# Second MLP layer of an FNet block as seven products, with the MLP in two passes and its activations in DRAM

## The chip, the cores and the metric

The kernel runs on one core of a Trainium2 chip. The core has TensorE (PE in the profile; PEld is its loading of weights), VectorE (DVE), ScalarE (ACT), GpSimd (POOL, which this kernel does not use for computing) and SyncE (SP, which here only issues DMAs). SBUF is the on-chip memory of 128 partitions; PSUM has eight banks, each of 512 float32 per partition, into which PE accumulates. The metric is the time of one execution in microseconds (us) on the device; lower is better.

## The reference

S = 2048 rows, D = 512, F = 1792, all float32.

```python
xn = layernorm(x)                       # over D
a = xn @ dft_hid_re.T;  b = xn @ dft_hid_im.T
s = dft_seq_re @ a - dft_seq_im @ b     # the FNet mixing
h = relu(xn @ w1 + b1) ** 2             # (2048, 1792)
out = x + s * silu(h @ w2 + b2)
```

## The kernel before

**Precision.** Every matmul operand is cut into a high part, rounded to PE's fast float32 type (`split`, L51: ACT copies, DVE subtracts the copy from the source), and a low part. A product is three passes, high x high, high x low, low x high (`PASSES`).

**Seven products.** A product of two operands, each cut 2 x 2 into blocks, takes seven block products in place of eight, if sums of blocks are formed first and the seven results are combined afterwards (`PRODUCTS`, `ORDER`). The kernel uses this for the sequence DFT of c = 2 to 7 (L476 to L516) and for the first MLP layer (`hidden`, L404), not for the second (`outer`, L439).

**Order of the work.** First layernorm, beside the plain sequence DFT of c = 0 and 1 (L286). Then six steps of c, each of eight j-steps: seven products of six matmuls of 256 columns (`mm`, L219), the moving operand being made two j-steps ahead (`prep`, `moving`); in j = 2, 3 the hidden DFT of the c before (`stage2`, L206), whose result y goes to DRAM. At j = 7 the seven PSUM banks are recombined by DVE into four blocks, cut into the buffers pq00 to pq11, from which `stage2` reads. Between, jobs prepare the weights (`make_w1`, `make_w2`): load, sums, cuts into the pq buffers, and DMA to DRAM.

Then the MLP in one pass over 28 units (c, p): four quarters c of 512 rows and seven pairs p of feature blocks. A unit is `hidden` (42 matmuls of 256 columns into four banks; recombination, Relu and square on DVE; cut on ACT and DVE) and, one unit behind, `outer`: 2 feature blocks x 4 row tiles x 3 passes = 24 matmuls of 512 columns, accumulated over all p in four PSUM banks. After the last p, `finish` adds b2, applies Silu, multiplies with y, adds x and writes the rows out. In the last quarter the end of the accumulation runs row tile by row tile (`REST`), the last row tile in two halves.

**What sets the order.** The code is traced in program order; a scheduler of the framework then puts each engine's instructions in an order of its own by their readiness, an instruction with earlier place first. Engines run their queues in order and wait on semaphores. A buffer is named by its tag: `buf("g1", ..., bufs=2)` is a tile in one of two buffers of tag g1, and a tile can be written when all readers of the tile that held the buffer are done, DMAs out of it included.

## Time and profile before

| | |
|---|---|
| median of three runs | 732.88 us (732.64 to 734.16) |
| the profiled execution | 733.41 us, span 731.5 us |
| PE busy | 721.0 us, 99% of the span |
| DVE busy | 547.6 us, 75% |
| ACT busy | 255.2 us, 35% |
| DMA | 133.70 MB, mean 183 GB/s |
| mean granted TensorE clock | 0.996 |

The span is the time from the first to the last instruction of the profiled execution, whose own time is 1.9 us longer. The DFT steps of c = 2 to 7 lie between 112.6 and 418.8 us and take 51 us each; the MLP runs from 418.8 us to the end. In rows of the profile, `out<-in` are tiles by their names with numbers left out, so `m<-g,xc` are the seven products of the DFT, `hps` those of the first MLP layer, `ops` the accumulators of the second; `128x512` is partitions by elements, x28 a count, then come the busy time in us, the mean of one in ns, and the idle time of the engine before them with what ended it.

### The profile page before, as it was taken

How to read it: one execution, taken by the hardware profiler on the slowest of the kernel's cores; microseconds unless marked ns; L12 is line 12 of the kernel's file. 1: busy time of each engine (PE TensorE's matmuls, PEld its weight loads, DVE VectorE, ACT ScalarE, POOL GpSimd, SP SyncE). 2: the span in 40 equal slices, each digit the busy share in tenths (PEclk: the TensorE clock that was granted, in tenths of full speed). 3: DMA queues.
4: the chain of work that ended last, by engine and by line, in shares of the span. 5: the costliest groups of instructions: out<-in, count | busy, mean ns of one | idle time of the engine just before them, and what ended most of it. 6: DMA issues, size and time to landing. Idle time of an engine off the chain costs nothing.

```text
span 731.5 us, 11771 instructions
## 1 busy us (share of the span) xinstructions
PE 721.0 (99%) x4687; PEld 654.1 (89%) x4687; DVE 547.6 (75%) x976; ACT 255.2 (35%) x386; POOL 0.2 (0%) x4
## 2 busy tenths in 40 slices
...
GB/s 301 231 88 86 211 77 87 148 298 117 234 255 91 288 188 111 307 137 127 289 135 149 360 425 288 151 167 86 231 207 139 95 226 184 143 73 288 116 116 59
DMA packets 43335, 133.70 MB, mean 183 GB/s; under 512 B 5008, under 2 KB 7312, under 8 KB 40592
## 3 DMA queue, kind: packets, MB, share of 16 engines
...
## 4 chain that ended last, share of the span: by engine, by line
PE 94%; DMA 2%; DVE 2%; ACT 1%; issue 1%; SPq 0%; DVEq 0%; ACTq 0%
PE m L219 33%; PE ops L441 19%; PE hps L414 17%; PE pq L309 13%; PE yps L206 12%; DMA w<-w2d 1%; DMA out<-fin 1%; DMA r<-in_ct 1%; DVE fin L457 0%; DVE fin L456 0%; ACT hh L52 0%; ACT g L52 0%; ACT z L455 0%; DVE z L454 0%; ACT xc L52 0%
## 5 line engine op out<-in xcount | busy, mean ns | idle before, releaser
L219 PEld LDWEIGHTS m<-g,xc 128*128 128x128 f32 x2016 | 242.6, 189 | 2.1
L219 PE MATMUL m<-g,xc 128*128 128x256 f32 x2016 | 243.2, 281 | 0.0
L441 PE MATMUL ops<-w,hh 128*128 128x512 f32 (+1 forms) x714 | 161.7, 381 | 0.4 <-ACT hh L52 0.3
L441 PEld LDWEIGHTS ops<-w,hh 128*128 128x128 f32 x714 | 126.5, 188 | 26.3 <-ACT hh L52 0.8
L414 PEld LDWEIGHTS hps<-xT,w 128*128 128x128 f32 x1008 | 123.3, 190 | 2.3
L414 PE MATMUL hps<-xT,w 128*128 128x256 f32 x1008 | 124.3, 281 | 0.0
L52 ACT ACTIVATE g<-r 128x768 fp32r<-128x768 f32 (+2 forms) x65 | 57.2, 888 | 128.9 <-PE m L219 99.3
L53 DVE TENSOR_TENSOR g<-r,g 128x768 fp32r<-128x768 f32 (+2 forms) x65 | 65.1, 1008 | 44.4 <-ACT g L52 44.2
L309 PE MATMUL pq<-g,xc 128*128 128x512 f32 x384 | 92.2, 400 | 3.7 <-ACT xc L52 3.7
L206 PE MATMUL yps<-wd,pq 128*128 128x512 f32 x384 | 94.1, 395 | 0.0
L309 PEld LDWEIGHTS pq<-g,xc 128*128 128x128 f32 x384 | 72.9, 190 | 22.4 <-ACT xc L52 4.5
L206 PEld LDWEIGHTS yps<-wd,pq 128*128 128x128 f32 x384 | 70.3, 188 | 15.1
L52 ACT ACTIVATE hh<-h 128x512 fp32r<-128x512 f32 x56 | 34.1, 630 | 116.4 <-DVE h L431 116.4
L53 DVE TENSOR_TENSOR g<-t,g 128x1024 fp32r<-128x1024 f32 x48 | 58.2, 1222 | 3.5 <-ACT g L52 3.3
L422 DVE SCALAR_TENSOR_TENSOR h<-hps,b1s,ht 128x256 f32<-128x256 f32 x28 | 13.5, 481 | 57.1 <-ACT ht L419 57.1
L52 ACT ACTIVATE g<-t 128x1024 fp32r<-128x1024 f32 x48 | 50.0, 1051 | 2.6 <-PE pq L309 2.6
L53 DVE TENSOR_TENSOR hh<-h,hh 128x512 fp32r<-128x512 f32 x56 | 36.8, 688 | 4.5 <-ACT hh L52 2.8
L431 DVE SCALAR_TENSOR_TENSOR h<-h 128x512 f32<-128x512 f32 x56 | 36.6, 685 | 0.3
L419 ACT ACTIVATE ht<-hps 128x256 f32<-128x256 f32 x28 | 10.7, 382 | 68.0 <-PE hps L414 68.0
L162 DVE TENSOR_TENSOR t<-r 128x512 f32<-128x512 f32 x48 | 32.5, 686 | 1.1 <-DMA r<-in_ct 0.8
L52 ACT ACTIVATE xT<-stage 128x768 fp32r<-128x768 f32 (+1 forms) x16 | 15.3, 955 | 45.8 <-DVE stage L248 28.2
L164 DVE TENSOR_TENSOR t<-r,t 128x256 f32<-128x256 f32 x48 | 19.8, 420 | 0.6
...
## 6 DMA issues: line engine op xcount, KB each, us to landing
r<-in_ct SPq DMA_DIRECT2D x63, 512.0 KB, 3.4
w<-w2d SPq DMA_DIRECT2D x28, 512.0 KB, 4.0
w<-w2d SPq DMA_DIRECT2D x14, 1024.0 KB, 4.8
w1d<-w1g SPq DMA_DIRECT2D x21, 512.0 KB, 4.2
...
w2d<-w2g SPq DMA_DIRECT2D x14, 512.0 KB, 5.2
...
stage<-in_xt SPq DMA_DIRECT2D x8, 512.0 KB, 5.2
```

The source lines that it names most:

```text
L52: cut[0] = nc.scalar.activation(hi, src, AF.Copy)
L53: return nc.vector.tensor_tensor(lo, src, hi.bitcast(F32), op=ALU.subtract)
L162: nc.vector.tensor_tensor(t[:, 0:2], r[:, I12:I12 + 1].to_broadcast([P, 2, CW]), r[:, I11:I22 + 1], op=ALU.subtract)
L164: nc.vector.tensor_tensor(t[:, 2], r[:, I22], t[:, 0], op=ALU.subtract)
L206: nc.tensor.matmul(ps, PQ[c, m, k // 2][:, a_, w:w + P], WD[m, k][:, b_, :], start=n == 0, stop=n == 2 * ND * 3 - 1)
L219: nc.tensor.matmul(ps[:, d * CW:(d + 1) * CW], w[:, a_, d * P:(d + 1) * P], mv(b_), start=first and d == 0 and (a_, b_) == (HI, HI), stop= ...
L309: nc.tensor.matmul(accs[k], w, g[:, b_, 2 * h:2 * h + 2], start=j == 0 and h == 0 and (a_, b_) == (HI, HI), stop=j == NJ - 1 and h == 1 an ...
L414: nc.tensor.matmul(M[n], W1[p][a][:, a_, q * P:(q + 1) * P], xT[c, q][:, b, b_], start=i == q == 0 and (a_, b_) == (HI, HI), stop=q == 1 a ...
L419: nc.scalar.activation(u, M[1], AF.Copy)
L422: nc.vector.scalar_tensor_tensor(h0[:, 0:256], M[2], c0, u, op0=ALU.add, op1=ALU.add)
L431: nc.vector.scalar_tensor_tensor(r, r, 0.0, r, op0=ALU.max, op1=ALU.mult)
L441: ins = nc.tensor.matmul(ps, H[c, f][:, a_, t * P:(t + 1) * P], W2[c, f][:, b_, cols], start=f == 0 and (a_, b_) == (HI, HI), stop=f == NF ...
```

## The change

- The second layer uses seven products too. Row halves and feature pairs of h, and feature pairs and column halves of w2, are the 2 x 2 blocks. Per unit: 7 products x 2 row tiles x 3 passes, 42 matmuls of 256 columns, into seven PSUM banks that accumulate over p; b2 is written by ACT into three of the banks before the accumulation (`bias`).
- The MLP runs in two passes. Pass one computes `hidden` for all 28 units, with Relu (with b1) and Square on ACT, and writes h to DRAM (HD), 512 KB a unit. For p = 6 (`EARLY`) the sums and cuts are made at once, and the cut operand is written from buffers g0a and g1a. Pass two loads each unit's h two units ahead (`outer_operand`), into g1a or g1b in turn, forms the sums, cuts all seven blocks into xc3, wd0 or wd1 in turn, and runs `outer`. A unit of p = 6 is loaded ready cut. W2 is read once, in the last quarter of pass one, into the xc buffers.
- Recombination (`combine`) works on pairs of products at once, so PSUM is split by tags: b3 (three banks), b2 (two), ba, bb and bc (one each), each a single buffer. DFT steps use b2, b3, ba, bb; `stage2` uses bc and comes in j = 1, 2.
- Weight jobs (`make_w`) are now 14 alike, at j = 2, 4, 6 (`JOBS`). They use a buffer e, which the recombination uses too.
- The halves of the next quarter's MLP input (`xt_half`) are made in three parts spread over units of pass one. At the end, the last quarter runs its last three p product by product.

```diff
-REST = NF - 3
+REST = NP - 3
+EARLY = (6,)
+JOBS = {2: (2, 4, 6), 3: (2, 4, 6), 4: (2, 4, 6), 5: (2, 4, 6), 6: (2, 4)}
...
-    acc = ctx.enter_context(tc.tile_pool(name="acc", bufs=8, space=bass.MemoryType.PSUM))
+    acc = ctx.enter_context(tc.tile_pool(name="acc", bufs=1, space=bass.MemoryType.PSUM))
...
-    def bank(name):
-        return acc.tile([P, 512], F32, tag="bank", name=name)
-    def t2k(name):
-        return pool.tile([P, 512], F32, tag="t2k", bufs=4, name=name)
+    def bank(tag, name):
+        n = {"b3": 3, "b2": 2}.get(tag, 1)
+        return acc.tile([P, n, 512], F32, tag=tag, name=name)
...
+    def sums_b(t, r):
+        nc.vector.tensor_tensor(t[:, 0:2], r[:, 0:1].to_broadcast([P, 2, 256]), r[:, 1:3], op=ALU.add)
+        nc.vector.tensor_tensor(t[:, 2], t[:, 1], r[:, 1], op=ALU.add)
+        nc.vector.tensor_tensor(t[:, 3], t[:, 2], r[:, 3], op=ALU.add)
+    def sums_a(t, a21, a11_a22, a11, a12):
+        nc.vector.tensor_tensor(t[:, 0:2], a21.to_broadcast([P, 2, 256]), a11_a22, op=ALU.subtract)
+        nc.vector.tensor_tensor(t[:, 2], t[:, 1], a11, op=ALU.subtract)
+        nc.vector.tensor_tensor(t[:, 3], t[:, 2], a12, op=ALU.add)
...
-        g0 = buf("g0", [P, 2, 3, CW], f"g0_{key}", F32R, bufs=2)
-        g1 = buf("g1", [P, 2, 4, CW], f"g1_{key}", F32R, bufs=2)
+        k = "ab"[turn[0] % 2]
+        turn[0] += 1
+        g0 = buf(f"g0{k}", [P, 2, 3, CW], f"g0_{key}", F32R)
+        g1 = buf(f"g1{k}", [P, 2, 4, CW], f"g1_{key}", F32R)
...
+    def banks(key):
+        m26, m753, m4, m1 = (bank(tag, f"m_{tag}_{key}") for tag in ("b2", "b3", "ba", "bb"))
+        return m26, m753, m4[:, 0], m1[:, 0]
+    def product(ms, n):
+        m26, m753, m4, m1 = ms
+        return {1: m1, 4: m4, 2: m26[:, 0], 6: m26[:, 1], 7: m753[:, 0], 5: m753[:, 1], 3: m753[:, 2]}[n]
+    def combine(e, ms):
+        m26, m753, m4, m1 = ms
+        pair = [P, 2, m1.shape[-1]]
+        nc.scalar.activation(e[:, 0], m1, AF.Copy)
+        nc.vector.tensor_tensor(e[:, 1:3], m26, e[:, 0:1].to_broadcast(pair), op=ALU.add)
+        nc.vector.tensor_tensor(e[:, 0:4:3], m753[:, 0:2], e[:, 2:3].to_broadcast(pair), op=ALU.subtract)
+        nc.vector.tensor_tensor(e[:, 2:4], m753[:, 1:3], e[:, 0:4:3], op=ALU.add)
+        if m4 is not None:
+            nc.vector.tensor_tensor(e[:, 0], m4, e[:, 0], op=ALU.subtract)
...
+        both = r.rearrange("p (k h) n -> p k (h n)", k=2)
+        for m, op in ((0, ALU.subtract), (2, ALU.mult)):
+            mr = xT["rows"][:, m:m + 2].rearrange("p h n -> p (h n)")[:, None, :]
+            nc.vector.tensor_tensor(both, both, mr.to_broadcast([P, 2, 512]), op=op)
+        yield
+        sums_b(t, r)
+        yield
+        g = xT[c, q] = buf(f"xc{q}" if c % 2 == 0 else f"wd{q}", [P, 2, 7, 256], f"xT{c}_{q}", F32R)
+        split(g[:, HI, 0:3], g[:, LO, 0:3], r[:, I11:I21 + 1])
+        split(g[:, HI, 3:7], g[:, LO, 3:7], t)
+        yield
...
+    def make_w(n, p):
+        e = buf("e", [P, 8, 256], f"w{n}raw{p}")
+        r, t = e[:, 0:4], e[:, 4:8]
+        nc.sync.dma_start(r, (w1, w2)[n][p])
+        if n == 0:
+            sums_a(t, r[:, 0:1], r[:, 1:4:2], r[:, 1], r[:, 2])
+        else:
+            sums_b(t, r)
+        for k, (first, count) in enumerate(((0, 2), (2, 1), (3, 2), (5, 2))):
+            g = buf(f"pq{k // 2}{k % 2}", [P, 2, count, 256], f"w{n}g{p}_{k}", F32R)
+            split(g[:, HI], g[:, LO], e[:, 1 + first:1 + first + count])
+            nc.sync.dma_start((W1D, W2D)[n][p][:, :, first:first + count], g.bitcast(F32))
+    work = [(0, p) for p in range(NP)] + [(1, p) for p in range(NP)]
+    jobs = {(c, j): work.pop(0) for c, js in JOBS.items() for j in js}
...
+    def load_w2(p):
+        t = W2[p] = buf(f"xc{(0, 1, 4, 5, 6, 7, 2)[p]}", [P, 2, 7, 256], f"w2_{p}", F32R)
+        nc.sync.dma_start(t.bitcast(F32), W2D[p])
...
+    def room(n, name):
+        return buf("r" if n % 4 < 3 else "sx", [P, 4, 256], name, bufs=3 if n % 4 < 3 else 1)
+    def hidden_sums(x_):
+        h = x_[:, 4:8]
+        sums_a(x_[:, 0:4], h[:, C12:C12 + 1], h[:, C11:C22 + 1], h[:, C11], h[:, C21])
+    def hidden(n, c, p):
+        if n % 2:
+            t, o = bank("b3", f"hps{n}_3"), bank("bc", f"hps{n}_1")
+            t = t.rearrange("p a (b n) -> p (a b) n", n=256)
+            ms = t[:, 0:2], t[:, 2:5], t[:, 5], o[:, 0, 0:256]
...
+            t, u, o = (bank(tag, f"hps{n}_{tag}") for tag in ("b2", "ba", "bb"))
+            t, u = (v.rearrange("p a (b n) -> p (a b) n", n=256) for v in (t, u))
+            ms = u, t[:, 0:3], t[:, 3], o[:, 0, 0:256]
+            order = ORDER if n else (1, 7, 5, 3, 4, 2, 6)
+        first = set()
+        for k in order:
+            a, b = W1_SLOT[PRODUCTS[k][0]], B_SLOT[PRODUCTS[k][1]]
+            share = next((pair for pair in ((2, 6), (7, 5), (3, 4)) if k in pair), k)
+            for q in range(2):
+                for a_, b_ in PASSES:
+                    nc.tensor.matmul(product(ms, k), W1[p][a][:, a_, q * P:(q + 1) * P], xT[c, q][:, b_, b],
+                                     start=share not in first, stop=q == 1 and (a_, b_) == (LO, HI),
+                                     skip_group_check=True)
+                    first.add(share)
+        early = buf("e", [P, 8, 256], f"h{c}_{p}") if p in EARLY else None
+        x_ = room(n, f"h{c}_{p}") if early is None else early[:, 4:8]
+        combine(x_, ms)
+        for f, s in ((2 * p, slice(C11, 4, 2)), (2 * p + 1, slice(C21, 4, 2))):
+            nc.scalar.activation(x_[:, s], x_[:, s], AF.Relu, bias=b1s[:, f:f + 1])
+        nc.scalar.activation(x_, x_, AF.Square)
+        if early is None:
+            nc.sync.dma_start(HD[c, p], x_)
+            return
+        hidden_sums(early)
+        for s, tag in ((slice(4, 7), "g0a"), (slice(0, 4), "g1a")):
+            g = buf(tag, [P, 2, s.stop - s.start, 256], f"h{tag}{c}_{p}", F32R)
+            split(g[:, HI], g[:, LO], early[:, s])
+            nc.sync.dma_start(HD[c, p][:, :, s], g.bitcast(F32))
+    def outer_operand(n, c, p):
+        g = buf(("xc3", "wd0", "wd1")[n % 3], [P, 2, 7, 256], f"g{c}_{p}", F32R)
+        if p in EARLY:
+            nc.sync.dma_start(g.bitcast(F32), HD[c, p])
+        else:
+            x_ = buf("g1" + "ab"[n % 2], [P, 8, 256], f"hr{c}_{p}")
+            nc.sync.dma_start(x_[:, 4:8], HD[c, p])
+            hidden_sums(x_)
+            split(g[:, HI], g[:, LO], x_[:, 0:7])
+        return g
+    BIASED = {2: 0, 5: 1, 4: 0}
...
+    def outer(m, n, g, p, cols=(0, 1)):
+        a, b = H_SLOT[PRODUCTS[n][0]], B_SLOT[PRODUCTS[n][1]]
+        for k in cols:
+            for a_, b_ in PASSES:
+                nc.tensor.matmul(m[:, k * 256:(k + 1) * 256], g[:, a_, a, k * P:(k + 1) * P], W2[p][:, b_, b],
+                                 start=p == 0 and k == 0 and (a_, b_) == (HI, HI) and n not in BIASED,
+                                 stop=p == NP - 1 and (a_, b_) == (LO, HI), skip_group_check=True)
...
+    def finish(c, e, first, count, cols=slice(0, 2)):
+        m, i = first // 2, first % 2
+        w = slice(cols.start * 256, cols.stop * 256)
+        z = e[:, first:first + count, w]
+        y, xr = (fin[c][2 * n + m][:, i:i + count, w] for n in range(2))
         nc.scalar.activation(z, z, AF.Silu)
-        nc.vector.tensor_tensor(y, z, y, op=ALU.mult)
-        nc.vector.tensor_tensor(y, y, xr, op=ALU.add)
-        nc.sync.dma_start(out[n * P:(n + 1) * P, cols], y)
+        nc.vector.tensor_tensor(z, z, y, op=ALU.mult)
...
+        if j in (1, 2):
+            stage2(c - 1, j - 1)
         if (c, j) in jobs:
-            make, arg = jobs[c, j]
-            make(arg)
+            make_w(*jobs[c, j])
         if j == NJ - 1:
-            u = t2k(f"m1_{c}")
-            nc.scalar.activation(u, M[1], AF.Copy)
-            c11 = t2k(f"c11_{c}")
-            nc.vector.tensor_tensor(c11, M[2], u, op=ALU.add)
-            nc.vector.tensor_tensor(u, M[6], u, op=ALU.add)
-            u3 = t2k(f"u3_{c}")
-            nc.vector.tensor_tensor(u3, M[7], u, op=ALU.add)
-            nc.vector.tensor_tensor(u, M[5], u, op=ALU.add)
-            c22 = t2k(f"c22_{c}")
-            nc.vector.tensor_tensor(c22, M[5], u3, op=ALU.add)
-            nc.vector.tensor_tensor(u, M[3], u, op=ALU.add)
-            nc.vector.scalar_tensor_tensor(u3, M[4], -1.0, u3, op0=ALU.mult, op1=ALU.add)
-            pq(c, 0, 0, c11)
-            pq(c, 1, 1, c22)
-            pq(c, 1, 0, u)
-            pq(c, 0, 1, u3)
+            e = buf("e", [P, 4, 512], f"c{c}")
+            combine(e, ms)
+            for m, dh, k in ((0, 0, C11), (1, 1, C22), (1, 0, C12), (0, 1, C21)):
+                pq(c, m, dh, e[:, k])
...
+    for n, (c, p) in enumerate(units):
+        hidden(n, c, p)
+        if n == 0:
+            stage2(NC - 1, 0)
+            stage2(NC - 1, 1, "ba")
+        if c == 0 and p + 4 < NP:
+            load_w1(p + 4)
+        if c + 1 < NTC and p < 6:
+            if p % 3 == 0:
+                making = xt_half(c + 1, p // 3)
+            next(making)
+        if c == NTC - 1:
+            if p == 0:
+                load_w2(0)
+                load_w2(1)
+            if p < 5:
+                load_w2(p + 2)
+    ready = {}
+    for n, (c, p) in enumerate(units[:2]):
+        ready[c, p] = outer_operand(n, c, p)
     for n, (c, p) in enumerate(units):
         last = c == NTC - 1
         if p == 0:
-            po = [(t, cols, bank(f"ops{c}_{t}_{cols.start}")[:, 0:cols.stop - cols.start])
-                  for t in range(TPC)
-                  for cols in ([slice(0, 256), slice(256, D)] if last and t == TPC - 1 else [slice(0, D)])]
-        if c == 0 and p + 4 < NP:
-            load_w1(p + 4)
-        if n + 1 < len(units):
-            load_w2(*units[n + 1])
-        if not last and p in (3, 4):
-            xt_half(c + 1, p - 3)
-        if p == 5:
-            for t in range(TPC):
-                load_fin(c * TPC + t)
-        if n + 1 < len(units):
-            if last and p + 1 >= NP - 2:
-                places = buf(f"xc{p + 3 - NP}", [P, 2, 2, TC], f"hh{p + 1}", F32R)
-                hidden(*units[n + 1], [places[:, i] for i in range(2)])
+            ms = banks(f"o{c}")
+            for k in BIASED:
+                if last and k == 4:
+                    m4 = bank("bc", "m4_last")[:, 0], ms[2]
+                    for i in range(2):
+                        bias(m4[i], k, slice(i, i + 1))
+                else:
+                    bias(product(ms, k), k)
+        if p == 2:
+            load_fin(c)
+        if n + 2 < len(units):
+            ready[units[n + 2]] = outer_operand(n + 2, *units[n + 2])
+        def add(k, p):
+            if last and k == 4:
+                for i in range(2):
+                    outer(m4[i], k, ready[c, p], p, (i,))
             else:
-                hidden(*units[n + 1])
-        for f in (2 * p, 2 * p + 1):
-            if not last or f < REST:
-                for t, cols, ps in po:
-                    tail = outer(ps, c, f, t, cols)
+                outer(product(ms, k), k, ready[c, p], p)
+        if not last or p < REST:
+            for k in ORDER:
+                add(k, p)
         if p == NP - 1:
-            z = buf("g0", [P, 3, 512], f"z{c}", bufs=2)
-            for t, cols, ps in po:
-                if last:
-                    for i in range(REST, NF):
-                        with tc.issue_after(tail.ins):
-                            tail = outer(ps, c, i, t, cols)
-                finish(ps, c * TPC + t, z[:, t] if t < 3 else t2k(f"z{c}_{cols.start}"), cols)
+            e = buf("e", [P, 4, 512], f"z{c}")
+            if last:
+                with tc.manual_schedule(engines={mybir.EngineType.PE}):
+                    for k in ORDER[:-1]:
+                        for i in range(REST, NP):
+                            add(k, i)
+                    for i in range(2):
+                        for f in range(REST, NP):
+                            outer(m4[i], 4, ready[c, f], f, (i,))
+                combine(e, (ms[0], ms[1], None, ms[3]))
+                finish(c, e, C11, 1)
+                for i in range(2):
+                    w = slice(i * 256, (i + 1) * 256)
+                    nc.vector.tensor_tensor(e[:, C21, w], m4[i][:, w], e[:, C21, w], op=ALU.subtract)
+                finish(c, e, C22, 2)
+                for i in range(2):
+                    finish(c, e, C21, 1, slice(i, i + 1))
+            else:
+                combine(e, ms)
+                done = c, e
+        elif c and p < 2:
+            finish(*done, (C21, C22)[p], 2)
```

204 lines of the change are left out of this document (67 added, 137 removed).

## The prediction

> **What bounds the kernel now.** The page first: busy shares, then the chain that ended last.
>
> ```profile
> span 731.5 us, 11771 instructions
> PE 721.0 (99%) x4687; PEld 654.1 (89%) x4687; DVE 547.6 (75%) x976; ACT 255.2 (35%) x386; POOL 0.2 (0%) x4
> PE 94%; DMA 2%; DVE 2%; ACT 1%; issue 1%; SPq 0%; DVEq 0%; ACTq 0%
> PE m L219 33%; PE ops L441 19%; PE hps L414 17%; PE pq L309 13%; PE yps L206 12%; DMA w<-w2d 1%; DMA out<-fin 1%; DMA r<-in_ct 1%; DVE fin L457 0%; DVE fin L456 0%; ACT hh L52 0%; ACT g L52 0%; ACT z L455 0%; DVE z L454 0%; ACT xc L52 0%
> ```
>
> PE is 94% of the chain: a matmul taken away is time won, and an idle microsecond on PE is time lost. There is almost no idle time to win. The change works on the 19% of L441. Its price per unit of two features comes from the chain in order of time (start, length):
>
> ```profile
> 625.99 5.04 PE hps L414 x42
> 631.03 5.60 PE ops L441 x24
> 636.63 4.98 PE hps L414 x42
> 641.61 5.53 PE ops L441 x24
> 647.14 4.91 PE hps L414 x42
> ```
>
> One unit has 42 hidden matmuls of 256 columns (4.91 to 5.04 us) and 24 outer matmuls of 512 columns (5.53 to 5.60 us).
>
> **1. The matmuls: minus 16 us.** A unit's outer work becomes 7 products x 2 halves x 3 passes = 42 matmuls of 256 columns: 10752 columns streamed in place of 12288, seven eighths. The price of 256 columns in a long run of them is in PE's order of time:
>
> ```profile
> 194.74 30.08 PE L219 MATMUL m<-g,xc 128*128 128x256 f32 x252
> ```
>
> 30.08 / 252 = 0.1194 us, so 42 are 5.01 us. A 512 costs 5.57 / 24 = 0.232 us, less than two 256s: of the eighth (0.70 us) only 5.57 - 5.01 = 0.56 us is left per unit. Times 28 units this is 15.7; the last quarter already has 84 matmuls of 256 columns in place of 42 wide ones, 84 x 0.1194 - 42 x 0.232 = 0.3 more. I take 16. Bounds: 28 x (5.53 - 5.04) = 14 and 28 x (5.60 - 4.91) = 19.
>
> **2. The seam between the passes: plus 20.** Pass one writes H to DRAM; pass two loads it, forms four sums and cuts seven blocks into high and low parts. In the steady state this hides: an operand is begun two units ahead. At the seam I see one that can't be. The first operand, (0,0), loads into buffer g1a. The tile allocated in g1a just before it in program order is that of the last hidden unit (3,6), which is in EARLY: its cut sums lie in g1a until their write to DRAM has landed. If a buffer's tiles take it in program order, the load waits for the end of that chain, which begins only when PE's last hidden matmul is done, and PE has nothing else left. Does the order hold? The four-buffer tag t2k shows it, in SP's and DVE's order of time:
>
> ```profile
> 79.02 1.09 SPq L353 DMA_DIRECT2D w1raw<-in_w  x2
> 147.32 0.58 SPq L369 DMA_DIRECT2D w2raw<-in_w  x1
> 155.03 5.32 SPq L152 DMA_DIRECT2D r<-in_ct  x2
> 164.00 0.33 SPq L353 DMA_DIRECT2D w1raw<-in_w  x1
> ```
> ```profile
> 152.82 0.68 DVE L53 TENSOR_TENSOR w2g<-w2raw,w2g 128x512 fp32r<-128x512 f32 x1
> 163.29 0.68 DVE L53 TENSOR_TENSOR pq<-c,pq 128x512 fp32r<-128x512 f32 x1
> ```
>
> A load from the inputs runs far ahead when its buffer is free: the w1raw at 79.02 was issued some 50 us before its place in the loop. Yet the next w1raw waited until 164.00, although all four t2k buffers were free from 153.5, when the last w2raw was cut, and SP was free after 160.4. In program order the four tiles of the quarter's recombination come between; the first of them was released at 163.97, and the load followed at 164.00. So tiles of a tag keep program order. The chain's durations:
>
> ```profile
> L52 ACT ACTIVATE g<-t 128x1024 fp32r<-128x1024 f32 x48 | 50.0, 1051 | 2.6 <-PE pq L309 2.6
> L53 DVE TENSOR_TENSOR g<-t,g 128x1024 fp32r<-128x1024 f32 x48 | 58.2, 1222 | 3.5 <-ACT g L52 3.3
> L52 ACT ACTIVATE g<-r 128x768 fp32r<-128x768 f32 x48 | 40.1, 844 | 103.5 <-PE m L219 99.3 <-issue 3.1 <-DMA r<-in_ct 1.0
> L53 DVE TENSOR_TENSOR g<-r,g 128x768 fp32r<-128x768 f32 x48 | 45.5, 956 | 40.7 <-ACT g L52 40.5
> L52 ACT ACTIVATE hh<-h 128x512 fp32r<-128x512 f32 x56 | 34.1, 630 | 116.4 <-DVE h L431 116.4
> L162 DVE TENSOR_TENSOR t<-r 128x512 f32<-128x512 f32 x48 | 32.5, 686 | 1.1 <-DMA r<-in_ct 0.8
> L164 DVE TENSOR_TENSOR t<-r,t 128x256 f32<-128x256 f32 x48 | 19.8, 420 | 0.6
> ```
> ```profile
> r<-in_ct SPq DMA_DIRECT2D x63, 512.0 KB, 3.4
> w<-w2d SPq DMA_DIRECT2D x14, 1024.0 KB, 4.8
> w1d<-w1g SPq DMA_DIRECT2D x21, 512.0 KB, 4.2
> w1b<-w1d SPq DMA_DIRECT2D x1, 1024.0 KB, 7.5
> ```
>
> From the last hidden matmul: the last double combination on DVE 0.69 (product 3 shares its bank with product 4, so it waits for both), two Relu of 512 elements on ACT 1.26, Square of 1024 1.05, three sums 0.69 + 0.42 + 0.42 = 1.53, the cut of 1024 on ACT 1.05 and DVE 1.22: 6.8. The write of 1 MB from g1a: no row has one, a 1 MB load took 4.8, which I take; bounds 4.2 (half as large a write) and 7.5 (a crowded load). The load of 0.5 MB 3.4: 15.0. Three sums again 1.53; the cut of 1792 elements, extended along the rows by 0.21 per 256 on ACT (0.63, 0.84, 1.05) and 0.27 on DVE, 1.68 and 2.02: 20.2. A dozen hand-overs between engines at some 0.05 add 0.6, and two or three matmuls run before the low parts arrive. I take 20, bounds 18 and 24. Next late would be operand (0,2), which takes g1a after (0,0): load, sums and cut end 3.4 + 1.5 + 3.7 = 8.6 us later, while PE has two units, 10 us. It just fits.
>
> **3. The clock after the seam: plus 1.7.** Windows at the start of the kernel (from:to length, PE, PEld, DVE, ACT, POOL, granted clock):
>
> ```profile
> 6.30:8.26 1.96, 0.00 (x1) 0.00 (x1) 1.49 (x3) 1.15 (x2) 0.00 (x0) 1.00 0.94 354
> 8.26:11.00 2.74, 2.74 (x8) 2.14 (x9) 2.60 (x10) 0.89 (x2) 0.00 (x0) 0.60 1.03 410
> 11.00:13.00 2.00, 2.00 (x8) 1.60 (x7) 2.00 (x3) 0.98 (x2) 0.00 (x0) 0.70 1.01 379
> 17.40:20.00 2.60, 2.60 (x11) 2.14 (x12) 2.60 (x8) 0.75 (x2) 0.00 (x0) 1.00 1.04 412
> ```
>
> After PE's pause of 1.96 us the clock was 0.60 and 0.70 for 4.7 us: 0.40 x 2.74 + 0.30 x 2.00 = 1.7 us lost. A pause ten times as long should cost at least that; I take 1.7, bounds 0 (some of it falls in the wait for the low parts) and 3.4. The Trainium skill (TensorE: Matmul & The Clock Gate, Part 1: The HAM clock gate) says that after an idle window of about 3.4 us the array restarts at half clock for about such a window; by that rule this term would be an estimated 1.7 and the sum the same. The trace agrees on the slow restart, but shows it after a pause shorter than the Trainium skill's window.
>
> **4. DVE in the DFT stage: plus 1.5.** Fourteen weight jobs (sums 1.53; cuts of 512, 512, 512 and 256 on DVE, 2.5) run in c = 2 to 6, three to a step of c, each behind the last in buffers e and pq. A step of c with two cheaper jobs, and its late part with two w1 jobs:
>
> ```profile
> 163.90:214.90 51.00, 51.00 (x386) 48.82 (x385) 40.47 (x64) 22.99 (x32) 0.00 (x0) 1.00 0.57 202
> 353.00:358.00 5.00, 5.00 (x44) 5.00 (x43) 5.00 (x8) 3.25 (x6) 0.00 (x0) 1.00 0.74 217
> 363.00:368.00 5.00, 5.00 (x45) 5.00 (x43) 4.84 (x8) 2.90 (x5) 0.00 (x0) 1.00 0.31 111
> ```
>
> The jobs of the first row's step were 7 cuts of 512 (0.69) and 5 operations of 256 (0.42), 6.9; the recombination changes from 7 x 0.69 to 3 x 1.22 + 0.69. DVE goes from 40.5 to 40.5 - 6.9 + 3 x 4.0 - 0.4 = 45.2 of 51 us: it still fits, but the end of a step is full already, and the recombination now queues behind the third job's buffer e. After stage two, five j-steps (25.3 us of PE) hold 5 x 3.7 of moving operands and up to 10.5 of jobs, 29. So a step may run late by 0 to 3.7 us, of which up to 3.6 is slack (products 7, 5, 3, 4 and the next 1 run before bank b2 is needed). I take 0.4 for each of four steps; bounds 0 (PE has no idle time there to win) and 8.
>
> **5. The rest: plus 1.5.** Pass one loses its outer work as cover: DVE has 7 x 2.5 of recombining (3 x 0.69 + 0.42), two input halves of 6.1 (2 x 1.22, sums 1.53, cuts 0.96 + 1.22) and 3.7 of EARLY work (1.53 + 0.96 + 1.22), 33.5 us in the 35.1 us of a quarter's 42 x 7 hidden matmuls. I take 0, bounds 0 and 4. In pass two it has six operands of 1.53 + 2.02, the recombination 4.4 and the finish 4 x 1.22, 30.6 of 35.1; the bias (ACT) must follow the recombination before a bank is used again: 0.5 in three seams of quarters, bounds 0 and 4. The tail:
>
> ```profile
> 716.13 10.19 PE L441 MATMUL ops<-w,hh 128*128 128x512 f32 x55
> 728.45 0.42 DVE L457 TENSOR_TENSOR fin<-fin 128x256 f32<-128x256 f32 x1
> ```
>
> Now DVE ends 2.5 us after PE. In the changed tail, two blocks finish at once (2 x 1.22 on DVE) ahead of the last halves, so some 3.5: plus 1, bounds -0.5 and 2.5. W2 is now read once, 7 x 1.75 MB, in place of once a quarter, and H is written and read in 0.5 MB tiles, one in 5 us at 3.4 to 4.2 each; nothing is taken for that.
>
> **The sum.** -16 + 20 + 1.7 + 1.5 + 1.5 = +8.7. The profiled execution took 733.41 us (span 731.5 and 1.9 around it), 0.5 above the median of 732.88. 733.4 + 8.7 - 0.5 = 741.6 us.
>
> **Rivals.** *The seam is hidden* (ends faster): the load of (0,0) gets g1a before unit (3,6) does, or its wait is otherwise met. Then only (0,1) is late, since its buffer g1b holds weights until the last hidden matmul: 3.4 + 1.5 + 3.7 = 8.6 less a unit of 5.0, some 3.6 us. 732.9 - 16 + 3.6 + 3 = 723.5; without any of the small losses 721. The change wins as soon as the seam costs under 13 us. The rows at 164.00 speak against it; for it speaks only that one case of an order is not all cases.
>
> *DVE becomes the bound in the DFT stage*: the jobs overrun their steps by the full 3.7 us, or the last does not clear e in time: plus 8 in place of 1.5, 748. For it: the full windows at 353 and 363. Against: those windows cost PE nothing, and DVE overlaps neighbours, 0.68 us operations starting 0.60 apart:
>
> ```profile
> 314.23 0.68 DVE L497 TENSOR_TENSOR c<-m,m 128x512 f32<-128x512 f32 x1
> 314.83 0.68 DVE L162 TENSOR_TENSOR t<-r 128x512 f32<-128x512 f32 x1
> ```
>
> *The products save nothing*: if the 42 weight loads set the pace (PEld fills 5.00 of 5.00 us at 353), a unit would cost what it did, and the sum is 757. The 0.1194 us is measured with those loads, so this is excluded to within a few per cent.
>
> **How the numbers follow.** Seam as summed 0.73 (735 to 748), hidden 0.16 (720 to 726), overload besides the seam 0.08 (748 to 755), products dear 0.03. The likeliest gives 741.6. The range goes from 721 to 750: it leaves out the last of the hidden case's low end and most of the overload, under 0.2. Changes of under 0.2% (1.5 us) can't be told from none here. Faster: 0.16 and a fourteenth of the first case, whose seam then costs 13 us or less, together 0.21; same 0.05; slower 0.74.
>
> **What would show it.** PE's groups: L441's 512s gone, 1176 matmuls of 256 at 0.119 each. One idle stretch of PE of 18 to 24 us some 140 us before the end, ended by ACT's or DVE's cut of operand (0,0), with the write and the load of H in sequence inside it, and a granted clock of about 0.5 to 0.7 behind it. In the DFT stage, idle time of PE below 0.5 us a step. The prediction is wrong if the load into g1a is issued before the last hidden matmul ends, or if PE waits at the seams of c for DVE by more than 2 us each.

## The result, and the profile after

The changed kernel takes 814.02 us (median of 4 runs, 811.18 to 814.93), the kernel before 733.05 beside it: a ratio of 1.1095 (95% interval 1.1065 to 1.1126). The forecast was 741.6 us and a range of 721 to 750; the time is 81 us above the kernel before, where 8.7 was forecast. The profiled execution took 811.18 us, its span is 809.4 us.

From the page of the changed kernel, the busy shares and PE's new group:

```profile
span 809.4 us, 12755 instructions
PE 727.1 (90%) x5149; PEld 680.5 (84%) x5149; DVE 577.3 (71%) x876; ACT 347.2 (43%) x470; POOL 0.2 (0%) x4
...
L503 PE MATMUL m_b_o<-w,g 128*128 128x256 f32 x840 | 110.2, 287 | 6.5 <-ACT m_b_o L496 6.5
```

PE was busy for 99% of the span and is now for 90%; no other engine is near full: most of PE's new idle time must be waiting. Windows cut the span at the stages (from:to length, PE, PEld, DVE, ACT, POOL busy, granted clock, DMA share, GB/s). First the kernel before: DFT stage, MLP, tail behind the last matmul.

```profile
112.60:418.80 306.20, 306.20 (x2305) 293.13 (x2304) 241.36 (x380) 134.89 (x183) 0.00 (x0) 1.00 0.55 196
418.80:726.30 307.50, 307.10 (x1940) 276.40 (x1938) 215.92 (x414) 68.70 (x118) 0.00 (x0) 1.00 0.51 178
726.30:731.50 5.20, 0.02 (x1) 0.00 (x0) 2.54 (x7) 0.51 (x2) 0.00 (x0) 0.76 0.43 153
```

The changed kernel: DFT stage, pass one, seam, pass two, tail.

```profile
113.20:435.90 322.70, 308.98 (x2305) 294.52 (x2304) 252.37 (x387) 142.80 (x199) 0.00 (x0) 0.99 0.57 203
435.90:605.20 169.30, 158.30 (x1226) 154.20 (x1224) 112.25 (x172) 91.11 (x133) 0.00 (x0) 0.96 0.65 251
605.20:630.50 25.30, 0.04 (x1) 0.04 (x1) 12.67 (x20) 10.25 (x12) 0.00 (x0) 0.60 0.71 272
630.50:800.30 169.80, 151.44 (x1176) 147.09 (x1176) 107.27 (x115) 51.35 (x43) 0.00 (x0) 0.95 0.49 166
800.30:809.40 9.10, 0.02 (x1) 0.00 (x0) 4.88 (x9) 1.67 (x3) 0.00 (x0) 0.73 0.25 86
```

The span grew by 77.9 us: 0.6 ahead of the DFT stage, 16.5 in it, 56.9 in the MLP (169.3 + 25.3 + 169.8 for 307.5) and 3.9 in the tail. Every stage has lost, not the seam alone. What PE waited for, in the changed kernel from the DFT stage on (total, times, longest):

```profile
PE m_bb_o L503 <- ACT g L65: 29.8, 4, 25.3
PE m_bb L264 <- ACT c L212: 7.5, 4, 2.1
PE m_bb_o L503 <- DVE g L66: 7.3, 10, 1.3
PE m_b_o L503 <- ACT m_b_o L496: 6.5, 5, 2.1
PE m_b L264 <- DVE c L213: 6.2, 4, 1.8
PE hps L459 <- DVE h L217: 3.9, 2, 2.1
PE hps_bb L459 <- ACT h L212: 3.9, 2, 3.3
PE hps_ba L459 <- DVE h L213: 2.2, 2, 2.1
```

The first line holds the seam (25.3). `c` is the recombination at the end of a DFT step (four steps, 13.7 us in all), `g` an operand of pass two, `m_b_o` the bias, `h` the recombination of a hidden unit.

### The profile page after: what moved, and what is told of

Read it like the earlier page. It is cut to its first block, busy times and chain, and to the rows that moved or that the text cites. A ratio compares the mean times of both kernels' runs of the same rounds, so it can differ in the third digit from the quotient of the medians.

```text
span 809.4 us, 12755 instructions
## 1 busy us (share of the span) xinstructions
PE 727.1 (90%) x5149; PEld 680.5 (84%) x5149; DVE 577.3 (71%) x876; ACT 347.2 (43%) x470; POOL 0.2 (0%) x4
## 5 line engine op out<-in xcount | busy, mean ns | idle before, releaser
L264 PE MATMUL m_b<-g,xc 128*128 128x256 f32 x1440 | 181.3, 281 | 6.2 <-DVE c L213 6.2
L264 PEld LDWEIGHTS m_b<-g,xc 128*128 128x128 f32 x1440 | 175.7, 189 | 7.7 <-issue 7.0
L503 PE MATMUL m_b_o<-w,g 128*128 128x256 f32 x840 | 110.2, 287 | 6.5 <-ACT m_b_o L496 6.5
L503 PEld LDWEIGHTS m_b_o<-w,g 128*128 128x128 f32 x840 | 106.1, 195 | 7.6 <-ACT m_b_o L496 7.5
L65 ACT ACTIVATE g<-hr 128x1792 fp32r<-128x1792 f32 x24 | 40.3, 1698 | 92.7 <-DVE hr L183 56.9
L361 PE MATMUL pq_b<-g,xc 128*128 128x512 f32 x240 | 67.2, 400 | 3.7 <-ACT xc L65 3.5
L459 PE MATMUL hps<-xT,w 128*128 128x256 f32 x504 | 66.8, 289 | 2.6 <-DVE h L217 2.1
L66 DVE TENSOR_TENSOR g<-t,g 128x1024 fp32r<-128x1024 f32 x48 | 58.7, 1223 | 14.0 <-ACT g L65 13.9
L459 PEld LDWEIGHTS hps<-xT,w 128*128 128x128 f32 x504 | 64.6, 198 | 3.3 <-DVE h L217 2.3
L66 DVE TENSOR_TENSOR g<-hr,g 128x1792 fp32r<-128x1792 f32 x24 | 48.0, 2023 | 17.4 <-ACT g L65 17.3
L503 PEld LDWEIGHTS m_bb_o<-w,g 128*128 128x128 f32 x168 | 25.4, 211 | 40.4 <-ACT g L65 30.6
L361 PEld LDWEIGHTS pq_b<-g,xc 128*128 128x128 f32 x240 | 45.4, 190 | 15.9 <-ACT xc L65 4.4
L65 ACT ACTIVATE g<-t 128x1024 fp32r<-128x1024 f32 x48 | 50.3, 1049 | 15.2 <-PE m_b L264 5.5
L264 PE MATMUL m_bb<-g,xc 128*128 128x256 f32 x288 | 43.5, 289 | 7.5 <-ACT c L212 7.5
L181 DVE TENSOR_TENSOR hr<-hr 128x512 f32<-128x512 f32 x24 | 16.6, 691 | 40.2 <-DMA hr<-hd 40.2
```

Of the source, the lines that this page charges most:

```text
L65: nc.scalar.activation(hi, src, AF.Copy)
L66: return nc.vector.tensor_tensor(lo, src, hi.bitcast(F32), op=ALU.subtract)
L181: nc.vector.tensor_tensor(t[:, 0:2], a21.to_broadcast([P, 2, 256]), a11_a22, op=ALU.subtract)
L264: nc.tensor.matmul(ps[:, d * CW:(d + 1) * CW], w[:, a_, d * P:(d + 1) * P], mv(b_), start=first and d == 0 and (a_, b_) == (HI, HI), stop= ...
L361: nc.tensor.matmul(accs[k], w, g[:, b_, 2 * h:2 * h + 2], start=j == 0 and h == 0 and (a_, b_) == (HI, HI), stop=j == NJ - 1 and h == 1 an ...
L459: nc.tensor.matmul(product(ms, k), W1[p][a][:, a_, q * P:(q + 1) * P], xT[c, q][:, b_, b], start=share not in first, stop=q == 1 and (a_, ...
```

## The experiments

All runs in one table, in microseconds of the profiled execution. A stage goes from its first matmul to the next stage's; in brackets PE's idle time in it, worked out as the sum of the gaps between matmuls. The changed kernel and e18 ran four times, the others once; the kernel before took 733.4 to 734.7 beside them (medians). The changed kernel's four runs lie 3.8 us apart, so a smaller difference between two single runs shows nothing by itself. Runs that leave a stage as the change made it show its own spread: 322.3 to 327.2 us for the DFT stage, 168.4 to 172.7 for pass one, 164.6 to 169.8 for pass two.

```
run                  time    DFT stage     pass one      seam   pass two
after               811.2   322.7 (13.7)  169.3 (11.0)   25.3  169.8 (18.4)
e1_seam             817.7   325.5 (15.3)  169.2 (10.8)   14.3  185.1 (27.8)
e2_jobs             828.3   305.9  (0.0)  170.3 (11.8)   61.8  167.0 (15.2)
e3_no_operands      785.8   327.2 (14.7)  169.2 (10.9)   23.8  142.2  (0.0)
e4_no_bias          813.1   325.3 (14.0)  172.7 (13.3)   25.2  166.4 (14.9)
e5_w2_late          816.5   326.2 (13.6)  169.4 (11.0)   13.5  182.5 (25.8)
e6_deeper           781.9   324.3 (14.8)  168.4 (13.0)   16.5  149.1  (5.7)
e7_jobs_235         815.3   327.6 (15.2)  170.2 (12.7)   25.3  169.1 (17.3)
e8_pass_one_light   798.4   322.3 (14.4)  162.8  (7.6)   25.2  164.6 (13.9)
e9_jobs_in_r        833.7   347.0 (23.1)  169.8 (11.2)   26.6  166.7 (15.3)
e10_deep_swap       779.5   326.4 (14.4)  169.4 (11.1)    5.8  154.6  (8.7)
e11_deep_swap_raw   763.1   325.3 (15.0)  158.9  (4.4)    6.3  149.4  (3.7)
e12_all_mends       786.3   345.8 (22.1)  156.5  (3.5)   16.1  144.1  (0.5)
e13_jobs_spread     766.5   305.9  (0.0)  176.6 (16.3)   17.7  143.2  (0.5)
e14_first_loads     763.3   305.9  (0.0)  178.7 (18.1)    6.7  148.5  (3.1)
e15_gpsimd          772.1   305.8  (0.0)  187.5 (22.6)    8.1  147.9  (2.4)
e16_jobs_on_act     755.0   311.4  (1.9)  156.6  (3.5)   17.9  143.4  (0.5)
e17_spread_light    746.5   305.9  (0.0)  162.4  (8.0)    2.8  149.5  (3.8)
e18_seven_rooms     762.7   324.6 (14.0)  154.1  (1.3)    9.1  150.0  (4.6)
```

### The first four: one suspect each

**e1_seam.** Unit (3,6) writes its H to DRAM raw (not summed and cut) like the other units.

```diff
-EARLY = (6,)
+EARLY = [(c, 6) for c in range(3)]
```

> Edit: the last hidden unit (c = 3, p = 6) is no longer written ready cut from g0a and g1a but raw, like the others; nothing else. Theory (the load of operand (0,0) waits for g1a): the 25.3 us idle stretch of PE between the passes shrinks to 3 to 9 us, since then only (0,1) is late (its g1b holds weights until the last hidden matmul), and the time falls from 811-815 to 788-797. Rival (the stretch comes from the backlog of w2 loads on the DMA engines, or from the first operands' own loads): the stretch stays at 15 us or more, the time above 800.

The seam fell by 11.0, to 14.3 us, and pass two grew by 15.3: the kernel is no faster. (In pass two PE waits 26.7 us for operands' cuts where the changed kernel waits 11.8; why so much more, this run doesn't show.) The rest of the seam is another wait, in SyncE's and VectorE's order of time:

```profile
597.38 0.32 SPq L484 DMA_DIRECT2D hr<-hd  x1
```
```profile
618.27 0.69 DVE L181 TENSOR_TENSOR hr<-hr 128x512 f32<-128x512 f32 x1 [5.86 <-DMA hr<-hd]
```

The first operand's load of 0.5 MB was issued 10 us before the last hidden matmul, and its sums began 20.9 us later, ended by the load. Seven loads of W2, 1.75 MB each, were issued ahead of it, the last at 595.4, and the DMA engines moved some 400 GB/s until about 619.

**e2_jobs.** Two weight jobs in a DFT step, the last four behind units (3,0) to (3,3).

```diff
-JOBS = {2: (2, 4, 6), 3: (2, 4, 6), 4: (2, 4, 6), 5: (2, 4, 6), 6: (2, 4)}
+JOBS = {2: (2, 4), 3: (2, 4), 4: (2, 4), 5: (2, 4), 6: (2, 4)}
+            if p < len(work):          # c == NTC - 1
+                make_w(*work[p])
```

> Edit: two weight jobs in each DFT step c = 2 to 6 (j = 2, 4) in place of three; the last four w2 jobs move to the last quarter of pass one. Theory (the third job holds buffer e until after the recombination wants it): PE's 13.7 us of idle time at the ends of c = 2 to 5 fall below 3, the half-clock window behind the first of them goes, and the time falls by 12 to 17 to 795-802; pass one may give 0 to 4 of it back. Rival (the recombination in pairs over banks b2 and b3 is late by itself): over 8 us stay.

The DFT stage is back at 305.9 us with no idle time: the third job is the whole of its loss. But the four jobs follow each other through buffer e, the early cut of (3,6) waits behind them for the same buffer, and the seam grew to 61.8. I had taken the end of pass one to be free for them.

**e3_no_operands.** The first three operands are used over and over.

```diff
-            ready[units[n + 2]] = outer_operand(n + 2, *units[n + 2])
+            ready[units[n + 2]] = outer_operand(...) if n == 0 else ready[units[n - 1]]
```

> Edit: pass two makes only its first three operands and uses them again for the other 25 units, so loads of H, sums and cuts are left out there (the second layer's result is not the reference's). Theory (the making of operands on ACT and DVE is what stops PE in pass two, at the quarter ends too, because its 2 us cuts stand before the recombination): of the 18.2 us of idle time in pass two less than 4 stay, the half-clock windows there go, pass two falls from 170 to about 143 to 147 us, and the time to 784-790. Rival (the ends of the quarters wait for recombination and bias by themselves): the three ends keep some 8 us and their half-clock windows, the time is 792-800.

```profile
632.80:775.00 142.20, 142.17 (x1176) 141.97 (x1176) 37.68 (x34) 16.85 (x22) 0.00 (x0) 0.98 0.23 73
```

Pass two without the making of operands runs its 1176 matmuls without a gap. The stalls at the ends of the quarters, which I had put down to recombination and bias, are gone too, though both are still done.

**e4_no_bias.** The bias isn't written into the banks; the first matmul of a bank starts its accumulation instead.

```diff
-                    bias(product(ms, k), k)
```

> Edit: b2 is left out: no write of the bias into the three banks, the first matmul of each bank starts the accumulation. Theory (at a quarter's end the chain recombination, then bias, then matmul is one step too long): the 6.5 us that PE waits for the bias fall to 1 to 4, since the bank must still be recombined first, and the time falls by 2 to 7. Rival (the recombination alone sets the end): no more than 1 us is won.

The total didn't fall, and pass two is 3.4 us shorter, no more than it varies by in runs that leave it as it was. So the bias costs at most a small part of the 30 us that pass two had lost, though PE's wait for it read 6.5: it was the last of a queue, not its cause.

### Pass two and the seam

**e5_w2_late.** As e1, with W2's last three loads written into pass two.

```diff
-            if p < 5:
+            if p < 2:
                 load_w2(p + 2)
+        if n < 3:                      # pass two
+            load_w2(n + 4)
```

> Unit (3,6) leaves its H raw, as in the run e1_seam, and besides three of the seven loads of W2 (1.75 MB each) are moved from the end of pass one into pass two, behind the first operands. Backlog theory: in e1_seam the load of operand (0,0) was issued at 597.4 and its sums began at 618.3, 21 us for 0.5 MB, because the W2 loads stood before it in the DMA engines; with three of them gone it lands within 8 us of its issue and the seam falls from 14.3 to 2 to 8 us (operand (0,1) still waits for the buffer that holds the last W1: 3.4 + 1.5 + 3.7 less a unit of 5.0). Rival, the chain on DVE and ACT (recombination of the last units, Relu, Square) holds the operand: the seam stays at 12 to 15. Pass two: if operands taken with two buffers can't get ahead, it stays near 185; if the late start alone kept it there, near 170.

A miss, and an empty one: the seven loads were issued when they were in e1 (the last at 597.4, 12 us before the last hidden matmul in both), since the scheduler puts a transfer where its buffer is free, not where it is written. It says nothing against the backlog.

**e6_deeper.** Raw H tiles load four units ahead into the buffers that H had in pass one.

```diff
...
-            x_ = buf("g1" + "ab"[n % 2], [P, 8, 256], f"hr{c}_{p}")
-            nc.sync.dma_start(x_[:, 4:8], HD[c, p])
-            hidden_sums(x_)
-            split(g[:, HI], g[:, LO], x_[:, 0:7])
+            h = raw.pop((c, p))        # room(n), loaded at unit n - 4
+            t = buf("t", [P, 4, 256], f"ht{c}_{p}", bufs=2)
+            sums_a(t, h[:, C12:C12 + 1], h[:, C11:C22 + 1], h[:, C11], h[:, C21])
+            split(g[:, HI, 4:7], g[:, LO, 4:7], h[:, 0:3])
+            split(g[:, HI, 0:4], g[:, LO, 0:4], t)
...
```

> In pass two the raw H tiles are loaded four units ahead into the four buffers that pass one used for H, not two ahead into the buffers in which the sums are formed; the cut into high and low parts is one of 768 and one of 1024 in place of one of 1792. Everything else is as changed. Theory of two buffers: load 3.4 + sums 1.5 + cut 3.7 = 8.6 us for each buffer against 10 us for two units, so any crowded load makes PE wait; with four, PE's idle time in pass two falls from 18.4 to under 6 us, its half clock from 17 to under 7, and pass two from 170 to 146 to 155. At the seam the first load no longer waits for g1a, only for the W2 loads before it: 25.3 falls to 8 to 15. Total 780 to 795. Rival, queueing on DVE and ACT (the operand's sums and cuts stand ahead of the recombination at the ends of the quarters): the idle time there (1.8 to 2.7 us each) stays and pass two stays above 160.

```profile
PE m_bb_o L510 <- ACT g L65: 16.6, 1, 16.6
PE m_bb_o L510 <- DMA g<-hd: 5.7, 1, 5.7
```

Pass two fell by 20.7 us, with VectorE doing more, not less (112.2 us for 107.3). The two lines are all that PE waits for in this run's pass two and seam: the seam, and one early operand, 1.75 MB in one load. In the changed kernel VectorE's first sum of an operand had stood 40.2 us for its load:

```profile
L181 DVE TENSOR_TENSOR hr<-hr 128x512 f32<-128x512 f32 x24 | 16.6, 691 | 40.2 <-DMA hr<-hd 40.2
```

The cut was also split in two here; the shares of the two aren't told apart.

**e10_deep_swap.** As e6; W2's last two blocks and the operands exchange buffers, so that two loads of W2 can't be issued before the last hidden unit ends.

```diff
-        t = W2[p] = buf(f"xc{(0, 1, 4, 5, 6, 7, 2)[p]}", ...)
+        t = W2[p] = buf(("xc0", "xc1", "xc4", "xc5", "xc6", "wd0", "wd1")[p], ...)
-        g = buf(("xc3", "wd0", "wd1")[n % 3], [P, 2, 7, 256], f"g{c}_{p}", F32R)
+        g = buf(("xc7", "xc2", "xc3")[n % 3], [P, 2, 7, 256], f"g{c}_{p}", F32R)
```

> As e6_deeper, and the buffers of W2's last two blocks and of the operands are exchanged, so that two loads of 1.75 MB can only be issued once the last hidden unit is done (they are needed some 25 us later) and the first operands' buffers are free two units earlier. (In e5_w2_late the loads were written further back but issued at the same times as before, so the backlog was not changed there.) Backlog theory: the first H tile then lands before the last hidden matmul and the seam falls from 16.6 to under 8 us; total 768 to 776. Rival, the chain of unit (3,6) on DVE and ACT (recombination, sums, two cuts) stands ahead of operand (0,0): the seam stays at 12 to 17.

The seam fell from 16.5 to 5.8, though unit (3,6) is still cut early: the W2 backlog held it. 5.5 of the 10.7 came back in pass two (3.0 of it idle time, with a wait of 2.8 us before the second operand, the rest longer matmuls), and 3.1 in the two stages ahead, which is within their spread. So the total fell by 2.4 only, 3.5 less than the least I expected.

**e11_deep_swap_raw.** As e10, and no unit is cut in pass one.

```diff
-EARLY = (6,)
+EARLY = ()
```

> As e10_deep_swap, and no unit cuts its H in pass one (EARLY is empty); all 28 operands are made in pass two. Theory that VectorE's queue makes pass one wait: 3.7 us less in each quarter, pass one falls from 168 to 158 to 164; the seam has no chain of a cut in it and falls to 2 to 6 us; in pass two VectorE has 34 us of work in 35, the idle time there lies between 2 and 10 us (the 5.7 us that PE waited for the last early operand in e6_deeper go). Total 752 to 766. Rival, VectorE becomes the bound of pass two: it takes over 152 us and the total stays above 768.

As expected in every stage but the seam (6.3, expected 2 to 6): pass one fell by 10.5, the wait for the early operand is gone, and VectorE with 123 of 149 us isn't the bound of pass two. At 763.1 us, 48 of the 78 us between the profiled executions are back.

### The DFT stage and pass one

**e7_jobs_235.** The jobs stand behind j = 2, 3 and 5.

```diff
-JOBS = {2: (2, 4, 6), 3: (2, 4, 6), 4: (2, 4, 6), 5: (2, 4, 6), 6: (2, 4)}
+JOBS = {2: (2, 3, 5), 3: (2, 3, 5), 4: (2, 3, 5), 5: (2, 3, 5), 6: (2, 4)}
```

> The three weight jobs of each step of c stand behind j = 2, 3 and 5 in place of 2, 4 and 6. Nothing else. Theory of the buffer: only the end of the third job, which must leave e before the first recombining copy, makes PE wait; then PE's idle time in the DFT stage falls from 13.7 to under 3 us and the stage from 322.9 to 306 to 310, and the total to 797 to 802. Rival, VectorE has simply more work than the five steps of j behind stage two hold (29 of 25 us): the idle time stays above 9 us wherever the jobs stand, or shows in the middle of a step.

No gain: 327.6 us is no less than what the stage takes untouched. The third job doesn't start where it is written, but when the job before it has left e. One step of the changed kernel (load, then the cuts, then the copy that opens the recombination):

```profile
154.13 0.56 SPq L400 DMA_DIRECT2D w0raw<-in_w  x1
```
```profile
159.62 0.94 ACT L65 ACTIVATE w0g<-w0raw 128x512 fp32r<-128x512 f32 x2
160.46 1.05 ACT L65 ACTIVATE g<-t 128x1024 fp32r<-128x1024 f32 x1
161.42 0.61 ACT L65 ACTIVATE w0g<-w0raw 128x512 fp32r<-128x512 f32 x1
163.21 0.63 ACT L65 ACTIVATE w0g<-w0raw 128x512 fp32r<-128x512 f32 x1 [1.18 <-issue]
163.74 0.83 ACT L65 ACTIVATE g<-r 128x768 fp32r<-128x768 f32 x1
164.48 1.04 ACT L65 ACTIVATE g<-t 128x1024 fp32r<-128x1024 f32 x1
165.50 0.60 ACT L212 ACTIVATE c<-m_bb 128x512 f32<-128x512 f32 x1
```
```profile
166.15 1.12 PE L264 MATMUL m_bb<-g,xc 128*128 128x256 f32 x4 [1.84 <-ACT c L212]
```

PE was done at 164.30 and needs bank m_bb back. The job's last low part on VectorE ended at 165.47, the copy into e (the last ScalarE line) began at 165.50.

**e8_pass_one_light.** The normalisation of x transposed is left out for c = 1 to 3.

```diff
-        for m, op in ((0, ALU.subtract), (2, ALU.mult)):
+        for m, op in ((0, ALU.subtract), (2, ALU.mult)) if c == 0 else ():
```

> For the columns c = 1 to 3 the normalisation of x transposed (two VectorE operations of 1024 elements per half, 6 x 2.44 = 14.6 us in all) is left out, so the MLP works on unnormalised values there. Theory that VectorE's queue makes pass one wait (33.5 of 35.1 us by the sum, 97 to 100% busy in 470 to 500): PE's idle time in pass one falls from 11.0 to under 3 us, the half clock from 13.7 to under 4, pass one from 169 to 154 to 158, the total to 799 to 804. Rival, the H tiles' buffers (the recombining copy waits until an earlier H tile has landed in DRAM): pass one stays above 165.

Between the two: pass one fell by 6.5 us for 13.2 less on VectorE. Its queue is part of the wait. (Pass two fell by 5.2 with no edit in it, within its spread.)

**e9_jobs_in_r.** The jobs use the moving operands' buffers r and t in place of e.

```diff
-        e = buf("e", [P, 8, 256], f"w{n}raw{p}")
-        r, t = e[:, 0:4], e[:, 4:8]
+        r = buf("r", [P, 4, 256], f"w{n}raw{p}", bufs=3)
+        t = buf("t", [P, 4, 256], f"w{n}t{p}", bufs=2)
```

> The weight jobs take their raw block and their sums from the buffers of the moving operands (r and t) and no longer from e, so that e has only the recombination in the DFT stage; three jobs a step as changed, nothing else. Theory of the buffer e: each job holds e for some 12 us (load landed 5.5 us after its issue, then sums and cuts), the third can't end before the step does, and the first recombining copy waits for it: without that, PE's idle time in the DFT stage falls from 13.7 to under 3 us, the stage from 322.9 to 306 to 310, the total to 797 to 802. Rival, VectorE is full at the end of a step (three jobs of 4.0 us): the idle time stays above 9 us. A third outcome, the moving operands now come late because the jobs take their buffers: idle time spread over the steps, not at their ends.

The third outcome, and dear: the stage takes 24 us more. What PE waits for has changed:

```profile
PE m_bb L264 <- DVE g L66: 12.8, 7, 2.8
PE m_b L264 <- DVE g L66: 3.6, 6, 1.0
```

The waits for `c` are gone, so e was what held the recombination; now the moving operands are late. **e12_all_mends**, e11 and e9 together, therefore lost as well:

> e11_deep_swap_raw and e9_jobs_in_r together. If the losses lie one behind another and don't depend on each other, the total is that of e11_deep_swap_raw less what e9_jobs_in_r gains on the changed kernel, within 3 us: some 737 to 750. The eighth of the second layer's products (16 us) beats the kernel before only if what is left of the stalls is under 16 us: I expect it not to, by a chance of two in three.

A miss: 786.3 us, 23 more than e11. The DFT stage is 20.5 longer, as in e9, and the seam 9.8, of which more at e14.

**e13_jobs_spread.** As e11, with two jobs a step and the other four in pass one behind units 6, 13, 20 and 23, now that e is free there.

```diff
+JOBS = {2: (2, 4), 3: (2, 4), 4: (2, 4), 5: (2, 4), 6: (2, 4)}
         hidden(n, c, p)
+        if n in (6, 13, 20, 23):
+            make_w(*work.pop(0))
```

> As e11_deep_swap_raw, with two weight jobs in a step of c, and the other four (W2's last blocks) in pass one behind the hidden units 6, 13, 20 and 23, where buffer e is now free. If the third job of a step is what costs the DFT stage its 17 us (e2_jobs) and e2_jobs only lost them again because four jobs stood at the end of pass one behind the early cut's buffer e, the stage takes 306, pass one stays below 164 (four jobs of 4.0 us on VectorE beside 30 of 35 us a quarter), the seam below 10, and the total is 742 to 752. Rival, VectorE has no room for the jobs anywhere: pass one or the seam grow by 10 us or more and the total stays above 755.

The DFT stage gave back 19.4 us, pass one took 17.7 and the seam 11.4 (two loads of W2 went ahead of the first H tile, and pass two, better supplied, was 6.2 shorter), so by the numbers the rival came true. **e14_first_loads**, as e13 with the first two H tiles asked for behind units (3,4) and (3,5) and W2's last loads behind the fourth:

```diff
-            if p < 5:
+            if p < 3:
                 load_w2(p + 2)
+            if p in (4, 5):
+                outer_load(p - 4)
...
+        if n < 2:                      # pass two, behind outer_load(n + 4)
+            load_w2(n + 5)
```

> As e13_jobs_spread, and the loads of the first two H tiles stand behind units (3,4) and (3,5), the last two loads of W2 behind the first four H tiles. In e11_deep_swap_raw the first H tile was asked for at 596.9, after the last hidden matmul (596.7), since the DMA queue of SyncE waited for an H tile of pass one, and two W2 loads went between it and the second. If the queue's order makes what is left of the seam, the seam falls from 6.3 to under 3 and the 2.8 us before unit (0,1) go: the total is 5 to 9 below e13_jobs_spread. Rival, the recombination of unit (3,6) on VectorE and ScalarE stands ahead of the first operand (its sums began at 602.1, just behind the Square): the seam stays at 5 to 7.

The order of the queue made the 11 us that the seam had grown by: it fell by 11.0. Pass two, begun earlier, gave 5.3 back, pass one 2.1. What e11's seam had left stayed, 6.7 us where under 3 was expected and the rival had 5 to 7, and the total fell by 3.2, not 5 to 9. The first H tile was still issued only at 595.03 and took 7.2 us to land, so the load ended after the last hidden matmul (597.3); this run doesn't show the rival's chain to be the cause.

So e13's seam isn't the price of its four jobs. e12 and e16 have pass two and its loads as e11 has them, and there too SyncE happened to issue the two loads of W2 ahead of the first H tile, while in e11 the tile came 0.5 us ahead of them. First e16 (seam 17.9), then e11 (6.3):

```profile
582.57 0.80 SPq L425 DMA_DIRECT2D w<-w2d  x2
583.93 2.23 SPq L478 DMA_DIRECT2D hr<-hd  x2
```
```profile
596.86 0.38 SPq L482 DMA_DIRECT2D hr<-hd  x1
597.33 1.26 SPq L429 DMA_DIRECT2D w<-w2d  x2
```

The tile landed 16.0 us after its issue in e16, 5.2 in e11.

**e15_gpsimd.** As e14, with the normalisation on GpSimd.

```diff
-            nc.vector.tensor_tensor(both, both, ...)
+            (nc.gpsimd if c else nc.vector).tensor_tensor(both, both, ...)
```

> As e14_first_loads, with the normalisation of x transposed for the columns 1 to 3 on GpSimd in place of VectorE (14.6 us of VectorE's work in pass one). If VectorE's queue still costs pass one its idle time (4.4 us and one half-clock window in e11_deep_swap_raw, more with the four jobs), the idle time falls below 2 us and pass one to 152 to 156, the total by 3 to 8 from e14_first_loads. Rival, GpSimd is slow enough, or hinders VectorE enough, that the input halves come late: pass one gets longer, the total is above e14_first_loads.

Again the rival came true: pass one grew by 8.8.

```profile
L293 POOL TENSOR_TENSOR stage<-stage,stage 128x1024 f32<-128x1024 f32 x12 | 30.4, 2532 | 513.1 <-DMA stage<-in_xt 504.0 <-ACT h L466 8.6
```

2.53 us for what takes VectorE 1.22 in e14. The Trainium skill (GPSIMD Engine Reference, 4.1 Engine selection) puts two-input elementwise work on GpSimd at about half VectorE's speed; the trace agrees, at 2.1 times.

**e16_jobs_on_act.** As e11, and the weight jobs put nothing on VectorE.

```diff
-            sums_a(t, r[:, 0:1], r[:, 1:4:2], r[:, 1], r[:, 2])
...
-            split(g[:, HI], g[:, LO], e[:, 1 + first:1 + first + count])
+            for part_ in (HI, LO):
+                nc.scalar.activation(g[:, part_], r[:, 0:count], AF.Copy)
```

> As e11_deep_swap_raw, but the fourteen weight jobs put nothing on VectorE: the four sums are left out and both halves of a weight block are copies of the raw block by ScalarE, so both layers multiply with wrong weights. Loads, writes, buffer e and the three jobs a step are as they were. Theory that VectorE's work at the end of a step (three jobs of 4.0 us) makes PE wait: the DFT stage falls from 325.3 to 306 to 309, the total to 743 to 747. Rival, the load of a job that can only start when the job before it has left e (5.5 us each) sets the end of the third job: the stage stays above 315.

The stage fell by 13.9 us and its idle time from 15.0 to 1.9, with the loads and the buffer as they were: VectorE's share of the jobs is what makes the third one end late, by its place in VectorE's queue or by its length in the job's own chain; the run doesn't tell these apart. (The stage is 5.5 above e2's, though only 1.9 of it is idle; the rest I can't place.)

**e17_spread_light.** As e14, without the normalisation for c = 1 to 3.

> As e14_first_loads, with the normalisation of x transposed left out for the columns 1 to 3 (as in e8_pass_one_light, so the MLP works on unnormalised values there), 14.6 us less on VectorE, about what the four moved weight jobs put there. Theory that VectorE has no room in pass one: its 178.7 us go back to 157 to 164, the total to 741 to 750. Rival, since VectorE is busy only 112 of those 179 us: the copy that opens a recombination waits in ScalarE's queue until an earlier H tile has landed in DRAM (23.8 us of waits in e14_first_loads), and VectorE and PE's banks behind it; then pass one stays above 170.

Pass one fell by 16.3 us for 13.6 less on VectorE, as the theory of VectorE's room has it. The windows of pass one, first e14, then this run:

```profile
418.60:597.30 178.70, 160.51 (x1226) 155.32 (x1224) 112.48 (x181) 91.12 (x137) 0.00 (x0) 0.95 0.69 259
```
```profile
421.00:583.40 162.40, 154.45 (x1225) 150.64 (x1224) 98.85 (x169) 91.15 (x139) 0.00 (x0) 0.99 0.78 290
```

Yet VectorE is busy for 63% of the longer one. Not its mean load but its queue at certain places makes PE wait, and I can't say which place.

**e18_seven_rooms.** As e11, with seven buffers for the H tiles of pass one.

```diff
-        return buf("r" if n % 4 < 3 else "sx", [P, 4, 256], name, bufs=3 if n % 4 < 3 else 1)
+        tag = ("r", "r", "r", "sx", "e", "g0a", "g1a")[n % 7]
+        return buf(tag, [P, 4, 256], name, bufs=3 if tag == "r" else 1)
```

> As e11_deep_swap_raw, with seven buffers in place of four for the H tiles of pass one (the three more lie in e, g0a and g1a, which are free there), so that a tile's write has 35 us in place of 20 to land. Theory of the H buffers: the copies' waits for landed H tiles (15.2 us in e11_deep_swap_raw) go to under 2, PE's idle time in pass one from 4.4 to under 1.5 with no half-clock window, pass one from 158.9 to 152 to 155, and the total to 756 to 760. Rival, VectorE's queue: the waits go and pass one stays at 157 to 160. Either way the kernel stays slower than before by more than 2%: the DFT stage still has its 325 us.

Pass one fell to 154.1 with 1.3 us idle: most of what e11 had left there was the wait for landed H tiles (15.2 us of ScalarE's waits, now 5.3, not under 2). The gain is 2.4 to 4.8 us, since e12 and e16, with e11's pass one, took 156.5 and 156.6. The seam and pass two took 3.4 of the 4.8 back, and the median of four runs, 764.2, isn't below e11's single 763.1. Against the kernel before the ratio is 1.0423 (1.0406 to 1.0440): no version with the whole computation beat it.

## Why the prediction was wrong

In its own terms, with what each measured (us):

```
term                                     forecast   bounds         measured
1 the matmuls                            -16        -14 to -19     -15.0
2 the seam                               +20        18 to 24       +25.3
3 the clock after the seam                +1.7      0 to 3.4       in 4 and 5
4 DVE in the DFT stage                    +1.5      0 to 8         +16.5
5 the rest: pass one                       0        0 to 4         +16.5
            pass two                      +0.5      0 to 4         +30.1
            tail                          +1        -0.5 to 2.5     +3.9
  ahead of the DFT stage                   -                        +0.6
sum                                       +8.7                     +77.9
```

Term 1: pass one takes 154.1 us at full clock in e18, 152.8 without its idle time; pass two in e3 takes 142.2, of which 5.0 at half clock, so 139.7 at full clock; 307.5 - 152.8 - 139.7 = 15.0. The measured 16.5 and 30.1 of term 5 are the stages less these.

**Right: the matmuls** and their price of 0.119 us, and **the seam's mechanism**: the first operand's load waits for the write out of g1a. The write, the loads, the operand's sums and cut, and PE's first matmul of pass two:

```profile
614.97 0.52 SPq L476 DMA_DIRECT2D hd<-hg1a  x1
622.25 10.56 SPq L484 DMA_DIRECT2D hr<-hd  x3
627.07 0.69 DVE L181 TENSOR_TENSOR hr<-hr 128x512 f32<-128x512 f32 x1
628.71 1.70 ACT L65 ACTIVATE g<-hr 128x1792 fp32r<-128x1792 f32 x1 [8.55 <-DVE hr L183]
630.46 0.79 PE L503 MATMUL m_bb_o<-w,g 128*128 128x256 f32 x2 [25.27 <-ACT g L65]
```

Of the three loads merged in the second line, the one issued at 622.67 waits for the semaphore of the write out of g1a, which had landed at 622.38. The seam's size was off by 5.3, in three places. The chain from the last hidden matmul to the write's issue took 9.8 us (605.19 to 614.97) for 6.8: four recombining operations stood in it, not one, and a bias on ScalarE. The write of 1 MB was given 4.8, and the load that waits for it was issued 7.7 us after it. From the load's issue to its sums were 4.4 us for 3.4. (The low parts of the cut, which the sum had counted, took PE no time: it started on the high parts.) "W2 is now read once", for which nothing was taken, is what filled the DMA engines: e1 and e10 show that its loads alone would have held the seam at some 14 us, had g1a been free. So the rival in which the seam hides had a second lock that I hadn't seen.

**Failed: term 4.** Its mechanism was named ("the recombination now queues behind the third job's buffer e") and then nearly waved away with "up to 3.6 is slack". There is none: the copy of product 1 is the first thing that the next step's first matmul waits for, and the copy stands behind e. Each of the four steps with three jobs lost 2.6 to 3.9 us of idle time (over the 2 us that the prediction had named as proof against it), and one a half-clock window. The bound of 8, not the 1.5, was the nearer figure; the row that spoke for it (VectorE at 5.00 of 5.00 us) was in the prediction. The rival "DVE becomes the bound in the DFT stage" is the one that came true, at twice its price (e2, e16): VectorE isn't busy throughout, but the jobs end too late.

**Failed: term 5.** I compared sums: 33.5 us of VectorE in a quarter's 35.1, 30.6 in pass two, and concluded 0 and 0.5. The sums were not even too low (VectorE is busy 28 us of a quarter in pass one). What failed is the step from "it fits" to "it is hidden". In pass one a bank comes free only when the recombination has had its turn on ScalarE and VectorE, behind the input halves (e8), the early cut (e11) and H tiles that haven't landed (e18). In pass two the operands were ready only just in time (e3 without their making: no idle time), since a buffer's round of load, sums and cut took 8.6 us, my own figure, of the 10 that two units give; "it just fits" had no room for a load that takes more than the 3.4 us it was given (median 4.4 in the changed kernel's pass two; with loads asked for earlier, e6, PE no longer waits for the operands that are made there).

**Failed: term 3** as a term of the seam alone. Half clock comes after short waits too (below): 34 us of it stand in the DFT stage and the two passes, which costs up to 17 us.

**The sign** was right, and the seam alone would have made it so: with its 25.3 the change would cost 10 us. The other 68 come from work beside PE that the sums had called hidden.

Open: which place in VectorE's queue makes pass one wait, why matmul time itself grows by some 2 to 4 us in places, beyond what the clock explains (e10, e16), how e6's gain divides between deeper loads and smaller cuts, and the tail's 2.9 us beyond the forecast.
